# 1/den sent to the channels through DRAM, a narrow Gram tail and token sums, and a new order, in a kernel that joins a long convolution and a linear attention block

## The chip, the cores and the metric

One Trainium2 chip, one core. The metric is the device time of one execution in microseconds. Five engines run side by side, each through its own list of instructions in order: TensorE (PE in the profile; its weight loads are shown as PEld), VectorE (DVE), ScalarE (ACT), GpSimd (POOL) and SyncE (SP), which here issues every DMA. Matmul results go to PSUM, eight banks that this kernel uses as four pairs; an evicting instruction on ACT or DVE copies them to SBUF.

## The reference

Two independent parts, whose outputs stand side by side. `S = 2048` tokens, `D = 576` channels, 32 heads of 18 channels, all inputs bf16.

```python
# part A
k_shift = sum over t of k_pad[:, t:t+S, :] * shift_k[:, ks-1-t]        # 4 taps
kv = k_shift * v
y  = irfft(rfft(kv, 2S) * rfft(ssm_k, 2S))[:S] + kv * ssm_D            # causal convolution
A  = q * y
# part B
q, k, v = split(x @ wqkv)                                              # 32 heads of 18
phi = lambda t: where(t > 0, t + 1, exp(t)) + 1e-6
kv  = einsum("bhsd,bhse->bhde", phi(k), v)
z   = phi(k) summed over tokens
num = einsum("bhqd,bhde->bhqe", phi(q), kv)
den = einsum("bhqd,bhd->bhq", phi(q), z)[..., None] + 1e-6
B   = (num / den) joined over heads @ wo
```

## The kernel before

Part A is cut into five chunks of channels (four of 128, one of 64). A chunk's convolution is two stages of small Fourier matmuls over 16 x 128 token indices, forward for the taps (`h`) and for `kv` (`u`), a product, and two stages back. In the names of the order list: `hl`/`hd`/`hT` load a chunk of `ssm_k`, add `ssm_D` to its first tap and transpose it (on TensorE, or by a copy and a DMA transpose); `cv` is the four-tap shift and the multiply by `v`, on DVE or POOL; `h1`/`u1` are the first forward stage, `ht`/`ut` a DMA transpose of its result, `h2`/`u2` the second stage; `pX`, `pT`, `pS`, `pA` the complex product (`N` in place of an engine drops a sum, and `i1` then carries one more plane of matmuls); `i1`/`i2` the stages back, `i2` multiplying by `q` on DVE; `st` the store.

Part B: `xl` loads x, `xd` transposes it; `k` and `q`/`qt` project and apply phi (exp on ACT, min and max on DVE) into `pk` and into `pqT` (channels 0 to 511 by tokens) and `pq4` (channels 512 to 575, two token groups on the two halves of the partitions). Instead of projecting v, the kernel makes the Gram product `GT = x^T phi(k)` (`G.0` to `G.4`, 16 token blocks each), then `kv` from `wv^T GT`, kept block diagonal by head, then `M = kv wo` (`M.0` to `M.4`), so that the output is `(phi(q) / den) @ M` (`o`, eight units of two 128-token blocks). `G.4` has 64 channels of x and a column of ones (`x_sb` is 577 wide, unit `one`), so that its 65th row holds the token sums z. `den` multiplies phi(q) by z spread over heads, adds epsilon and takes the reciprocal on DVE: `rden`, 32 heads on each of four partition groups (one group of 512 tokens each). `bc.c.gg` spreads it from heads to channels: two matmuls with the selecting matrix `esel` (built by eight POOL selects in `hc`), then one DVE instruction that computes `(pqT + eps) * spread` straight from PSUM; `bt` does the same for `pq4`.

The order of everything is written out by hand in the list `ORDER`: units run in that order on every engine's own list, and the digits behind a slash name the PSUM bank pair or the SBUF slot that a tile takes. A unit that waits, waits in its place, and so does whatever is queued behind it on that engine. SP issues all loads, stores and DMA transposes in the same order.

The lines that the change touches: the constants (L103 to L114, L132, L205 to L212, L233), the x tile (L308 to L316), L602, `b_G` (L619), `b_kv` (L631), `b_M` (L653), `b_den` (L668), `b_bc` (L690), `b_bt` (L699), `b_out` (L708). L292 and L294 are the helper that evicts on ACT and on DVE.

## Time and profile before

| | us |
|---|---|
| three runs, median (lowest to highest) | 171.63 (169.48 to 173.51) |
| the profiled execution, its own time | 171.69 |
| its span, first to last instruction | 170.0 |
| granted TensorE clock, mean | 0.976 of full |
| ACT busy | 123.6 (73%) |
| POOL busy | 93.1 (55%) |
| DMA queue of SP: 31.61 MB | 84.8% of 16 engines' span |

The busy time of TensorE comes from records of pipelined matmuls: the duration in a row of one matmul (379 ns for 512 columns) is longer than its spacing in a stream, so prices are read from start to start. A row of the timeline shows the start, the duration (of the whole run where it says x16), engine, line, operation, output and inputs, and in brackets the idle time before it and what ended it.

### The profile page before, as it was taken

Reading aid. Unit: us, or ns where it says so; the run is one execution under the profiler, and the core shown is the slowest. Engines: PE = TensorE matmul, PEld = TensorE weight load, DVE = VectorE, ACT = ScalarE, POOL = GpSimd, SP = SyncE. Lnnn points to the kernel's source line nnn. Section 1 sums busy time; section 2 is a strip of 40 time slices with the busy share of each in tenths; the row PEclk is TensorE's granted clock in tenths of the full one; section 3 lists DMA queues with packets and bytes.
Section 4 is the critical chain, followed back from the end, with each engine's and each line's share of the span. In section 5 each row is a group of like instructions: output and inputs, shape, how many; then the busy total and the mean of one; then the engine's idle time right before and its main releaser. Section 6 shows DMA issues by size and latency. Waiting matters only on the chain. (4 is left out here: it accounts for less than half of the span.)

```text
span 170.0 us, 4572 instructions
## 1 busy us (share of the span) xinstructions
PE 154.7 (91%) x1975; PEld 97.2 (57%) x1975; DVE 146.2 (86%) x163; ACT 123.6 (73%) x142; POOL 93.1 (55%) x80
## 2 busy tenths in 40 slices
PE   7598999999999899999959999978999989969990
PEld 7496554565634573545565578665546555647650
DVE  7787499988899899999999968696998989998861
ACT  3459998887898878505679967978998777675111
POOL 7996109459919799997000029999994050505000
PEclk9969999999999999999978999999999999999998
DMA  3899949999989699899997611984669999580586
GB/s 124 254 357 304 260 98 230 320 182 183 217 208 156 152 230 167 149 259 242 245 233 191 123 28 25 184 188 139 127 123 183 222 242 142 155 267 9 183 271 133
DMA packets 79564, 31.90 MB, mean 188 GB/s; under 512 B 55294, under 2 KB 78840, under 8 KB 79544
## 3 DMA queue, kind: packets, MB, share of 16 engines
q1 hardware_dynamic: 79544, 31.61, 84.8%
q8 instruction: 15, 0.25, 0.6%
q14 instruction: 5, 0.04, 0.1%
HBM read 15.48 MB, written 4.72 MB: 119 GB/s over the span
## 5 line engine op out<-in xcount | busy, mean ns | idle before, releaser
L544 POOL TENSOR_TENSOR T<-T 128x1024 bf16<-128x1024 bf16 x5 | 11.3, 2255 | 21.0 <-DVE T L541 20.9
L424 PE MATMUL k_ps<-wqk,xT 128*128 128x512 bf16 (+1 forms) x160 | 20.9, 286 | 0.0
L625 PE MATMUL g_ps<-pk,x_sb 128*128 128x65 bf16 (+3 forms) x160 | 20.6, 287 | 0.3 <-ACT SU L292 0.3
L504 PEld LDWEIGHTS <-G 128*128 128x128 bf16 x320 | 17.6, 97 | 5.0 <-issue 3.6
L433 PE MATMUL q_ps<-xT,wqk 128*128 128x512 bf16 x80 | 18.4, 379 | 0.0
L463 DVE TENSOR_TENSOR at<-at 128x2048 bf16<-128x2048 bf16 (+1 forms) x13 | 17.0, 1308 | 1.0 <-POOL at L462 0.5
L462 POOL TENSOR_TENSOR at<-k,Wj 128x2048 bf16<-128x2048 bf16 (+1 forms) x4 | 14.3, 3580 | 6.1 <-DVE at L463 3.4
L292 ACT ACTIVATE Cu<-s_ps 128x1024 bf16<-128x1024 f32 (+1 forms) x17 | 15.8, 978 | 1.9 <-PE s_ps L504 1.7
L718 PE MATMUL o_ps<-wo_M,pqT 128*128 128x512 bf16 (+1 forms) x128 | 17.0, 286 | 0.1
L292 ACT ACTIVATE SU<-s_ps 128x1024 bf16<-128x1024 f32 x16 | 15.8, 1021 | 1.7 <-PE s_ps L527 1.3
L625 PEld LDWEIGHTS <-x_sb 128*128 128x128 bf16 (+1 forms) x160 | 10.9, 101 | 10.8 <-issue 1.5
L292 ACT ACTIVATE ob<-o_ps 128x576 bf16<-128x576 f32 x12 | 7.4, 650 | 13.2 <-PE o_ps L723 13.2
L424 PEld LDWEIGHTS <-xT 128*128 128x128 bf16 x160 | 10.9, 98 | 10.4 <-issue 0.5
L561 PE MATMUL i_ps<-W,T 64*128 64x128 bf16 x160 | 12.4, 234 | 4.3 <-ACT wv_GT L629 1.9
L292 ACT ACTIVATE T<-s_ps 128x1024 bf16<-128x1024 f32 x16 | 15.8, 1019 | 0.7 <-PE s_ps L527 0.6
L292 ACT ACTIVATE Ch<-s_ps 128x1024 bf16<-128x1024 f32 (+1 forms) x16 | 14.6, 948 | 2.3 <-PE s_ps L504 2.3
L292 ACT ACTIVATE V<-i_ps 128x1024 bf16<-128x1024 f32 x14 | 13.6, 1027 | 1.1 <-DMA Ctu<-Cu 0.9
L417 DVE SCALAR_TENSOR_TENSOR pk<-pk,k_ps 128x576 bf16<-128x576 bf16 x16 | 11.9, 753 | 2.9 <-ACT pk L416 2.9
L416 ACT ACTIVATE pk<-k_ps,neg 128x576 bf16<-128x576 f32 x16 | 11.8, 745 | 3.6 <-PE k_ps L424 3.4
L539 POOL TENSOR_TENSOR X<-SU,T 128x2048 bf16<-128x2048 bf16 x3 | 13.0, 4331 | 1.6 <-ACT SU L292 1.6
L718 PEld LDWEIGHTS <-pqT 128*128 128x128 bf16 x128 | 8.7, 98 | 8.5 <-issue 0.5
L462 DVE TENSOR_TENSOR at<-k,Wj 128x2048 bf16<-128x2048 bf16 (+1 forms) x11 | 13.1, 1187 | 0.2 <-POOL at L463 0.2
(144 smaller groups left out, 363.2 us busy)
## 6 DMA issues: line engine op xcount, KB each, us to landing
x_sb<-in_B_x_dram SPq DMA_DIRECT2D x4, 576.0 KB, 7.4
out_dram<-ob SPq DMA_DIRECT2D x8, 288.0 KB, 2.3
h_sb<-in_A_ssm_k_dram SPq DMA_DIRECT2D x4, 512.0 KB, 5.1
k<-in_A_k_dram SPq DMA_DIRECT2D x2, 1024.0 KB
v<-in_A_v_dram SPq DMA_DIRECT2D x2, 1024.0 KB
q<-in_A_q_dram SPq DMA_DIRECT2D x2, 1024.0 KB
out_dram<-q SPq DMA_DIRECT2D x2, 1024.0 KB
wqk<-in_B_wqkv_dram SPq DMA_DIRECT2D x2, 576.0 KB, 8.2
```

The lines of the kernel that those rows point to most:

```text
L292: nc.scalar.activation(out=out, in_=in_, func=ACT.Copy)
L416: nc.scalar.activation(out=out_ap, in_=ps_ap, func=ACT.Exp, bias=K.neg1[0:n, :])
L417: nc.vector.scalar_tensor_tensor(out=out_ap, in0=out_ap, scalar=1.0, in1=ps_ap, op0=ALU.min, op1=ALU.max)
L424: nc.tensor.matmul(ps[:, n0:n1], lhsT=xT[r // 4][:, t, rr * 128:(rr + 1) * 128], rhs=wqk[:, t, D + n0:D + n1], start=(t == 0), stop=(t == 4))
L433: nc.tensor.matmul(ps[:, j, :], lhsT=wqk[:, t, 128 * c:128 * c + 128], rhs=xT[g][:, t, :], start=(t == 0), stop=(t == 4))
L462: on[0].tensor_tensor(out=t_, in0=kk[:, 3 - stage:19 - stage], in1=wb(stage), op=ALU.mult)
L463: on[1].tensor_tensor(out=a_, in0=a_, in1=t_, op=ALU.add)
L504: nc.tensor.matmul(ps[:, bi, 0:dc], lhsT=K.G[ri][:, b, :], rhs=xf(b), start=True, stop=True)
L539: e.tensor_tensor(out=s['X', hf][:], in0=s['SU', hf][:], in1=t[:, :, ::-1, :], op=ALU.mult)
L561: nc.tensor.matmul(ps[:, r, g, :], lhsT=s[key, hf][64 * r:64 * r + 64, z, x, 128 * g:128 * g + 128], rhs=K.W[64 * r:64 * r + 64, m, :], st ...
L625: nc.tensor.matmul(ps[0:fn, n0:n1], lhsT=x_sb[:, r, f0:f0 + fn], rhs=pk[:, r, n0:n1], start=(r == 0), stop=(r == 15))
L718: nc.tensor.matmul(ps[:, n0:n1], lhsT=pqT[:, c, r * 128:(r + 1) * 128], rhs=B['M'][:, c, n0:n1], start=(c == 0), stop=False)
```

## The change

It moves the spreading of 1/den off TensorE: `rden` is stored to a scratch tensor in DRAM (`rs`), and five loads (`bl`) read it back, each head's row repeated for its 18 channels, into two rotating buffers (the slots of `xT`, free by then); a DVE multiply of two SBUF operands (`bc`) follows. Epsilon is added to phi(q) beforehand (`ep`, four times on ACT, once on DVE). `esel` and its eight selects go, and `ones`. The Gram tail `G.4` has 64 columns, even token blocks on the lower half and odd ones on the upper half of the output partitions; the token sums are a unit of their own, `z`, in four 32-column tiles. The tail of `wv` is loaded twice so that the kv products run over 128 rows everywhere, and `M`'s second product over all rows of the next head chunk. An `f` behind a unit `o` runs its tail matmuls first.

`ORDER` is written anew. Units that now run otherwise: `hT.2` and `hT.3` by a POOL copy and a DMA transpose, `hT.4` on TensorE, `hT.1` evicted by ACT; nine sums dropped (`N`) in place of four; no `pX`, `pS` on POOL; all `o` evictions on ACT; 56 warm-up matmuls in place of 40. From the reciprocal to the first `o` the new list reads:

```
den/3 cv.3.3.PPD u2.2.0.1.A/11 pA.1.0.N u2.2.0.0.A/2 i1.1.0.1.A/00 ht.3.1/1 i1.1.1.1.A/1 i1.1.1.0.A/2 pX.2.1.D/0
i1.1.0.0.A/0 cv.4.0.D hT.4.D/12 cv.4.1.DP ht.3.0/0 rs h2.3.1.1.A/33 vl.2/1 u1.3.1.0.A/12 u1.3.1.1.A/0 u1.3.0.1.D/3
u1.3.0.0.A/1 i2.1.1/2 h2.3.1.0.A/0 pX.2.0.D/1 M.1.A/3 bl.2/1 bc.2.D bl.4/0 bc.4.D i2.1.0/1 pA.2.0.N h2.3.0.0.A/22
h1.4.0.0.A/00 pT.2.0.D h2.3.0.1.A/3 h1.4.1.0.A/2 ut.3.1/1 M.2.A/0 pS.2.0.N M.4.A/3 pT.2.1.D ut.3.0/0 cv.4.2.DD
h1.4.0.1.A/2 u2.3.1.0.D/11 u2.3.1.1.A/0 bl.3/1 bc.3.D pS.2.1.N bl.1/0 h1.4.1.1.A/3 pA.2.1.N M.3.A/2 i1.2.0.1.A/10
cv.4.3.PDD i1.2.0.0.A/3 pX.3.1.D/1 bc.1.D M.0.A/2 u2.3.0.0.A/00 i1.2.1.0.A/1 u2.3.0.1.A/3 ht.4.0/1 i1.2.1.1.A/2
u1.4.1.1.A/00 u1.4.0.0.D/1 bl.0/1 h2.4.0.1.A/13 bc.0.D u1.4.1.0.A/2 ql.1/0 u1.4.0.1.A/0 pX.3.0.D/0 pA.3.0.P
h2.4.0.0.A/1 ql.2/0 pT.3.0.D i2.2.1/3 pA.3.1.D pS.3.0.D ut.4.0/0 o.1.0.AAf/20
```

```diff
-    K.esel = cpool.tile([128, D], BF, name="esel")
...
-    K.onesr = cpool.tile([128, 8], BF, name="onesr")
...
+    K.onec = cpool.tile([128, 32], BF, name="onec")
...
-        nc.sync.dma_start(out=wg[0:64, 0, 4, :], in_=wqkv[512:576, 2 * D:3 * D])
+        for i in range(2):
+            nc.sync.dma_start(out=wg[64 * i:64 * i + 64, 0, 4, :], in_=wqkv[512:576, 2 * D:3 * D])
...
+    def evict_G(ps, out):
+        ex = ab.tile([128, 1], FP32, name="ex", tag="ex", bufs=2)
+        nc.vector.tensor_copy(out=ex[:], in_=ps[:, D:D + 1])
+        nc.scalar.activation(out=out, in_=ps[:, 0:D], func=ACT.Identity, bias=ex[:])
...
+                if t < 4:
+                    nc.tensor.matmul(ps[:, n0:n1], lhsT=x_sb[:, r, 128 * t:128 * t + 128], rhs=pk[:, r, n0:n1],
+                                     start=(r == 0), stop=(r == 15))
+                else:
+                    h = slice(64 * (r % 2), 64 * (r % 2) + 64)
+                    nc.tensor.matmul(ps[h, n0:n1], lhsT=x_sb[:, r, 512:576], rhs=pk[:, r, n0:n1], start=(r < 2),
+                                     stop=(r > 13))
+        evict_G(ps, B['GT'][:, t, :])
+
+    def b_z():
+        ps = psum.tile([128, 1024], FP32, name="zs_ps")
+        for n0, n1 in ((0, 512), (512, 577)):
+            for r in range(16):
+                j = 32 * (r % 4)
+                nc.tensor.matmul(ps[j:j + 32, n0:n1], lhsT=K.onec[:], rhs=pk[:, r, n0:n1], start=(r < 4), stop=(r > 11))
+        B['zs'] = ab.tile([128, D], BF, name="zs")
+        evict_G(ps, B['zs'][:])
...
-    def b_bc(c, gg):
-        ps = psum.tile([128, 2, 512], FP32, name="bc_ps")
...
+    def store_r():
+        B['rs'] = dpool.tile([32, 4, 512], BF, name="rscr")
+        nc.sync.dma_start(out=B['rs'][:].rearrange("h j n -> j h n"), in_=B['rden'])
+
+    def eps_q(c, eng='A'):
+        p = pqT[:, c, :] if c < 4 else pq4[:]
+        if eng == 'A':
+            nc.scalar.activation(out=p, in_=p, func=ACT.Identity, bias=K.epsc[:])
+        else:
+            e = nc.gpsimd if eng == 'P' else nc.vector
+            e.tensor_scalar(out=p, in0=p, scalar1=EPS, scalar2=None, op0=ALU.add)
+
+    def load_r(c):
+        t = B['bc', c] = ring([128, 5, 512], BF, "rb", "xT", 2)
+        jobs = [(0, 0, 4, min(128, D - 128 * c))]
+        if c == 4:
+            jobs = [(64 * i, PAIR[0][i], 2, 64) for i in range(2)]
+        for p0, j0, jn, n in jobs:
+            ch = 128 * c
+            end = ch + n
+            while ch < end:
+                h, e = divmod(ch, 18)
+                m, k_ = (1, min(18 - e, end - ch)) if e or end - ch < 18 else ((end - ch) // 18, 18)
+                src = B['rs'][h:h + m, j0:j0 + jn, :].rearrange("h j n -> h (j n)")
+                nc.sync.dma_start(out=t[p0:p0 + m * k_, 0:jn, :].rearrange("p j n -> p (j n)"),
+                                  in_=src.unsqueeze(1).to_broadcast([m, k_, 512 * jn]))
+                p0 += m * k_
+                ch += m * k_
+
+    def b_bc(c, eng='D'):
+        p, r = (pqT[:, c, :], B['bc', c][:, 0:4, :]) if c < 4 else (pq4[:], B['bc', c][:, 0:2, :])
+        if c < 4:
+            r = r.rearrange("p j n -> p (j n)")
+        (nc.gpsimd if eng == 'P' else nc.vector).tensor_tensor(out=p, in0=p, in1=r, op=ALU.mult)
```

More of the change, by code (lines that the diff above doesn't have):

```diff
@@ L311, in load_x @@
     def load_x(g):
[L312 to L315 removed]
+        nc.sync.dma_start(out=x_sb[:, 4 * g:4 * g + 4, :], in_=xv[:, 4 * g:4 * g + 4, :])
     def xt(g):
@@ L713, in b_out, with tail @@
-        for r in rs:
-            ps = psum.tile([128, 1024], FP32, name="o_ps")
-            pss.append(ps)
+        pss = [psum.tile([128, 1024], FP32, name="o_ps") for r in rs]
+        first = len(eng) > 2
+        def tail():
+            for n0, n1 in ((0, 512), (512, 576)):
+                for i in range(2):
+                    h = slice(64 * i, 64 * i + 64)
+                    nc.tensor.matmul(pss[i][:, n0:n1], lhsT=pq4[h, p, rr * 128:(rr + 1) * 128], rhs=B['M'][h, 4, n0:n1],
+                                     start=first, stop=not first)
@@ L725, in b_out @@
+        if not first:
+            tail()
+        if eng[2:] == 's':
+            evict(B['ob'][:, rs[0], :], pss[0][:, 0:D], eng[0])
+            nc.sync.dma_start(out=outB[:, rs[0], D:2 * D], in_=B['ob'][:, rs[0], :])
+            for n0, e in ((0, 'D'), (288, 'A')):
+                evict(B['ob'][:, rs[1], n0:n0 + 288], pss[1][:, n0:n0 + 288], e)
+            nc.sync.dma_start(out=outB[:, rs[1], D:2 * D], in_=B['ob'][:, rs[1], :])
+            return
         for i, r in enumerate(rs):
```

141 lines of the change are left out of this document (53 added, 88 removed).

## The prediction

> **What bounds the kernel now.** I read the page's busy times first, then the timeline of TensorE for the places where it stands still, then the waits that explain those places, and last the timeline of VectorE against the order list.
>
> ```profile
> span 170.0 us, 4572 instructions
> PE 154.7 (91%) x1975; PEld 97.2 (57%) x1975; DVE 146.2 (86%) x163; ACT 123.6 (73%) x142; POOL 93.1 (55%) x80
> 165.91 0.75 DVE ob L294
> ```
>
> Two engines are nearly full. No engine's sum alone is the time: TensorE (PE) and VectorE (DVE) hold each other up. The chain of waits ends with the last output eviction on DVE, and behind that only the store, until 170.0. Of TensorE's 15.3 idle us, some 4 lie at the end, where only the eviction and the store run. Two places before that matter for this change.
>
> The first is at 85 us:
>
> ```profile
> 83.62 1.18 PE L482 MATMUL hT_ps<-ident,h_sb 128*128 128x128 bf16 x16
> 86.73 0.25 PE L561 MATMUL i_ps<-W,T 64*128 64x128 bf16 x2 [1.94 <-ACT wv_GT L629]
> ...
> 90.22 4.17 PE L625 MATMUL g_ps<-pk,x_sb 128*65 128x512 bf16 x32
> 94.33 0.63 PE L527 MATMUL s_ps<-Cth,W 64*32 64x512 bf16 x16
> ...
> 140.04 0.23 PE L561 MATMUL i_ps<-W,T 64*128 64x128 bf16 x2
> 141.04 2.13 PE L718 MATMUL o_ps<-wo_M,pqT 128*128 128x512 bf16 x16
> ACT wv_GT L629 <- DVE ex L628: 9.6, 3, 5.9
> 75.19 1.54 POOL L109 TENSOR_SCALAR_AFFINE_SELECT esel<-esel 32x576 bf16<-32x576 bf16 x1
> 76.23 1.57 DVE L462 TENSOR_TENSOR at<-k,Wj 128x2048 bf16<-128x2048 bf16 x1
> 77.83 3.03 DVE L463 TENSOR_TENSOR at<-at 128x2048 bf16<-128x2048 bf16 x1
> 80.89 1.22 DVE L462 TENSOR_TENSOR at<-k,Wj 128x2048 bf16<-128x2048 bf16 x1
> ```
>
> TensorE waited 1.94 us for a Gram eviction on ScalarE (ACT), which itself waited up to 5.9 us for the one-column copy `ex` on DVE. DVE was late because its elementwise operations took 1.57 us and once 3.03 us where the same shape takes 1.22; the long ones stand beside GpSimd's `esel` selects, and the 3.03 beside another small GpSimd operation. After the wait the four i1 units (64 matmuls) from 86.73 to 90.22 took 3.49 us; two units of the same kind at 140.04 to 141.04 took 1.0, so four cost 2.0 at full speed. The place costs 1.94 + 1.5 = 3.4 us.
>
> The second is the stretch from the denominators to the first output block:
>
> ```profile
> 107.75 1.05 PE L672 MATMUL den_ps<-pqT,zsel 128*32 128x512 bf16 x16
> 109.26 0.62 PE L527 MATMUL s_ps<-Ctu,W 64*32 64x512 bf16 x16
> 109.75 0.76 DVE L686 TENSOR_SCALAR den_ps<-den_ps,ez 128x512 f32<-128x512 f32 x1
> 110.54 3.36 DVE L688 RECIPROCAL wo_M<-den_ps 128x512 bf16<-128x512 f32 x1
> ...
> 130.59 1.22 DVE L697 SCALAR_TENSOR_TENSOR pqT<-pqT,bc_ps 128x1024 bf16<-128x1024 bf16 x1
> 132.00 2.13 PE L718 MATMUL o_ps<-wo_M,pqT 128*128 128x512 bf16 x16
> ```
>
> The last multiply by 1/den ends at 131.81 and the first output matmul starts at 132.00: DVE's chain sets it, not TensorE's own work. So the span is three pieces: 109.26 us up to the end of `den` on TensorE, 22.74 us from there to the first `o`, and 38.0 us after it.
>
> **Up to `den`.** The tail of the Gram product ran 32 matmuls from 90.22 to 94.33, 4.1 us. In 64-column pairs it should take half:
>
> ```profile
> 53.43 1.27 PE L441 MATMUL qt_ps<-xT,wqk 128*64 128x512 bf16 x10
> 54.63 0.41 PE L527 MATMUL s_ps<-Ctu,W 64*32 64x512 bf16 x8
> 58.97 1.16 PE L482 MATMUL hT_ps<-ident,h_sb 128*128 128x128 bf16 x16
> 60.06 0.41 PE L527 MATMUL s_ps<-Ctu,W 64*32 64x512 bf16 x8
> ```
>
> Here ten 64-column matmuls of 512 took 1.20 us, 0.24 a pair, so two do run side by side: -2.05. The new token sums are 16 matmuls of 512 and 16 of 65 in 32-column tiles; the 16 of `den` took 0.98 us (107.75 to 108.73), and the 65-wide ones are taken at 0.02 each: +1.3. The head transposes of chunks 2 and 3 leave TensorE for a GpSimd copy and a DMA transpose: 58.97 to 60.06 is 1.09, 83.62 to 84.80 is 1.18, -2.27. One i1 pair gets a third plane because its subtraction is dropped (pS.0.1.N): two units at 0.5 / 2 more, about +0.4 rounded with its weights. Sum -2.6.
>
> The wait at 85 us should go. Without `esel` and with the `X` and `S` sums off GpSimd, the DVE stretches of five operations by 0.35 and one by 1.8 have no cause: DVE is some 3.5 us less behind, while the added `ex` copy is short. Count -3.4; both ends are 0 and -3.4. What covers this: `pq + eps` now runs on ScalarE (four times; one on DVE), which has idle time there (73% busy). If that cover is missing, the evictions of the Gram product queue behind it and the wait returns.
>
> ```profile
> 119.21 4.07 POOL L541 TENSOR_TENSOR T<-SU,T 128x2048 bf16<-128x2048 bf16 x1
> 120.96 4.64 DVE L697 SCALAR_TENSOR_TENSOR pqT<-pqT,bc_ps 128x1024 bf16<-128x1024 bf16 x4
> 1.15 4.18 PE L80 MATMUL warm_ps<-sm 128*128 128x128 bf16 x40 [1.15 <-DVE sm L82]
> ```
>
> The two GpSimd copies for the transposes may stretch DVE as the selects did. No row shows such a copy, so they cost 0 to +2.4 us (some seven operations by 0.35); I take 0, since four DVE operations beside GpSimd's 4.07 us product took 4.64, no more than without it. Sixteen more warm-up matmuls lie in the shadow of the first loads: 0, at most 16 x 4.18 / 40 = 1.7. The padded kv rows change no matmul's length: 0. The first piece becomes 109.3 - 6.0 = 103.3.
>
> **From `den` to the first `o`.** DVE's own queue counts here. Per operation:
>
> ```profile
> L695 PE MATMUL bc_ps<-wo_M,esel 32*128 32x512 bf16 x16 | 3.1, 384 | 0.0
> 88.08 1.22 DVE L460 TENSOR_TENSOR at<-k,Wj 128x2048 bf16<-128x2048 bf16 x1
> ...
> 95.21 1.21 DVE L462 TENSOR_TENSOR at<-k,Wj 128x2048 bf16<-128x2048 bf16 x1
> 131.73 0.68 DVE L462 TENSOR_TENSOR at<-k,Wj 128x1024 bf16<-128x1024 bf16 x1
> ...
> 134.38 0.69 DVE L463 TENSOR_TENSOR at<-at 128x1024 bf16<-128x1024 bf16 x1
> ```
>
> The spreading matmuls free 3.1 us of TensorE, and the four of the tail some 0.4, but TensorE isn't the bound here, so that alone gains nothing. Six full DVE operations from 88.08 to 95.21 are 1.19 each start to start, four half ones 0.66. Between the reciprocal and the first `o` the new order has 14 full ones (four of them the new multiplies, bf16 from SBUF) and 9 half ones: 16.7 + 5.9 = 22.6 us. With 0.2 of lead and 0.76 + 3.36 for the reciprocal the piece is 26.9 us against 22.74: **+4.2**. The multiplies themselves got cheaper (five of 5.4 us in place of nine of 11), but convolution, products and evictions of chunks 2 to 4 were moved in front of them.
>
> The added waits. The sync queue (SP) now stores 1/den, then loads it back in 15 pieces, and DVE waits for each chunk; queued behind a waiting multiply are the DVE products and the evictions that free PSUM banks, and TensorE waits for those.
>
> ```profile
> h_sb<-in_A_ssm_k_dram SPq DMA_DIRECT2D x4, 512.0 KB, 5.1
> out_dram<-ob SPq DMA_DIRECT2D x8, 288.0 KB, 2.3
> k<-in_A_k_dram SPq DMA_DIRECT2D x2, 22.5 KB, 1.6
> 112.98 3.32 SPq L617 DMA_DIRECT2D wo_M<-in_B_wo_dram  x5
> ```
>
> A 512 KB load lands 5.1 us after its issue; a smaller store, 2.3; an issue takes 3.32 / 5 = 0.66. First multiply: 2.3 + two issues 1.3 + 5.1 = 8.7 against 5 full and 3 half operations of cover, 7.9: wait 0.8. Chunk 3, whose buffer is freed by the first multiply: 1.3 + 5.1 = 6.4 against four full and three half, 6.7: none. Chunk 0, freed by chunk 3: 0.66 + 5.1 = 5.8 against two full and three half, 4.4: 1.4. Together **+2.2**; the ends are 0 and, with fewer DMA engines per load, 15 (below). TensorE's own work in the stretch is at most 22.7 - 3.5 and the 5.0 that are moved in (next part), 24.2 us of 29.1, so it will stand still about 5 us in it; the half-speed loss behind the 1.94 us wait was 1.5, and I take half of that, **+0.75**.
>
> The Trainium skill's page "TensorE: Matmul & The Clock Gate", Part 1, says the clock halves after an idle window of about 3.4 us and needs as long a busy one to come back: by it this loss would be an estimated 1.7 us in place of 0.75, and the trace's loss after only 1.94 us of waiting is earlier than the page has it.
>
> **From the first `o` on.** Ahead of it now lie eleven units that lay behind: two u2 and two h2, four u1 of chunk 4, two i1, one i2.
>
> ```profile
> 136.83 0.41 PE L527 MATMUL s_ps<-Ctu,W 64*32 64x512 bf16 x8
> 137.18 0.86 PE L504 MATMUL s_ps<-v,G 128*128 128x64 bf16 x16
> 137.97 0.41 PE L527 MATMUL s_ps<-Ctu,W 64*32 64x512 bf16 x8
> L292 ACT ACTIVATE ob<-o_ps 128x576 bf16<-128x576 f32 x12 | 7.4, 650 | 13.2 <-PE o_ps L723 13.2
> ```
>
> At 0.35, 0.40, 0.5 and an estimated 0.95 each that is 1.4 + 1.6 + 1.0 + 0.95: **-5.0**, hidden ahead of `o` by the DVE chain. The last pair of blocks is evicted by ScalarE twice, 1.3 us in place of 0.75: **+0.55**.
>
> Sum: -6.0 + 4.2 + 2.2 + 0.75 - 5.0 + 0.55 = -3.3, made against the profiled execution's 171.69 us (span 170.0 and 1.69 around it), which is also the median of the runs (171.63): **168.4 us**. DVE is left with eleven full and seven half operations behind the first `o`, 17.7 us of the 33.5, so nothing new should appear there.
>
> **Rivals.** *Everything hides* (0.24). The loads land under cover and TensorE's wait is split so that its clock holds: 168.4 - 2.2 - 0.75 = 165.4. For it: each cover misses by about 1 us only. Against: other transposes stand ahead in the same queue.
>
> *The loads come late* (0.20), the one that ends slower. Place: DVE at the first, third and last multiply. The main piece of a load reads six or seven head rows and repeats them 18 times; if so few rows use so few of the 16 DMA engines, the data part of 5.1 - 1.6 = 3.5 us grows by about 16/6 on 84% of the bytes (seven on 98%: the same 7.9), landing 9.5 us after issue. Waits: 5.2, 4.1 and 5.8, 15.1 in place of 2.2, 181.3 in all; with half the excess and the clock's whole loss, 175.6. I take 176.5. It is slower than before by 2% once the three waits exceed 9 us. For it: nothing in the old trace repeats rows like this.
>
> The Trainium skill's page "DMA: Bandwidth & Descriptors", section "Why a DMA increments its semaphore by 16 and not by 1", says a DMA uses the largest number up to 16 that divides the slowest dimension of both sides, here 6 or 7; at its 27 GiB/s per engine a load is an estimated 1.6 us longer, which alone would give about 173. No row here shows it.
>
> *The early gain doesn't come* (0.14). The wait at 85 us stays for want of DVE time: 168.4 + 3.4 = 171.8; if narrow tiles did not overlap either, 2.05 + 2.8 more, 176.7. The `qt` row speaks against the latter, so 172.5. That the change doesn't do what it says is this case.
>
> **How the numbers follow.** The forecast has 0.42, with its own range 166 to 171. About 2% (168.2 and 175.1) is what a measurement tells from no change; the forecast lies on that line, 0.20 of it faster and 0.22 the same. Faster: 0.20 + 0.24 = 0.44. Same: 0.22 + 0.14 + 0.02 of the late loads = 0.38. Slower: 0.18. The range runs from 163.5 (everything hides and the small gaps before `o` go too) to 176.5, which leaves out half of the late loads and a little below.
>
> **What would show it.** Right: `den` on TensorE ends near 103 to 105 us; DVE operations stay at 1.2 us between 60 and 85; the first `o` starts 29 us after `den`, and TensorE idles several us before it; the first and last multiplies wait a microsecond for DMA; 33 us follow. Wrong: Gram tail matmuls spaced as before; a half-speed stretch of i1 again; landings of the spread loads near 9 us; or a first `o` that starts earlier than DVE's list allows, which would mean the half operations are cheaper than 0.66.

## The result and the profile after

| | before | after |
|---|---|---|
| median of the runs, us | 170.78 (169.48 to 173.51, 4 runs) | 189.50 (188.21 to 189.79, 4 runs) |
| ratio, 95% interval | | 1.111 (1.100 to 1.122) |
| profiled execution, its own time, and span | 171.69, 170.0 | 189.79, 188.0 |

The forecast was 168.4 with a range to 176.5; the changed kernel is 11% slower. Ratios leave out executions that took over 1.5% longer than the fastest of the same kernel; medians and ranges hold all of them. From the page of the changed kernel:

```profile
span 188.0 us, 4745 instructions
PE 157.7 (84%) x2047; PEld 100.9 (54%) x2047; DVE 141.5 (75%) x158; ACT 128.9 (69%) x150; POOL 61.9 (33%) x64
...
PEclk9988999999999999999969999996579669789998
```

The engines have little more to do than before: TensorE is busy 3 us longer, part of it at a lower clock (PEclk is the granted clock in tenths of full speed), ScalarE 5 us longer, VectorE 5 and GpSimd 31 us shorter. The time went into waiting. The windows view, cut where the prediction cut the span (end of `den` on TensorE, first full output matmul, end), shows in which piece. Columns: stretch, its length, then busy time and count of each engine, granted clock, DMA share, GB/s. The kernel before:

```profile
0.00:109.26 109.26, 102.15 (x1135) 64.58 (x1136) 95.51 (x113) 83.19 (x92) 66.04 (x71) 0.97 0.91 198
109.26:132.00 22.74, 20.67 (x390) 12.90 (x381) 19.91 (x18) 20.43 (x26) 20.01 (x7) 1.00 0.79 152
132.00:170.00 38.00, 31.87 (x467) 19.75 (x464) 30.73 (x33) 19.94 (x27) 7.02 (x3) 0.98 0.75 179
```

The changed kernel, the same view:

```profile
0.00:111.15 111.15, 100.66 (x1171) 62.70 (x1172) 94.02 (x115) 86.89 (x95) 50.06 (x60) 0.97 0.98 209
111.15:151.35 40.20, 27.86 (x536) 20.79 (x528) 26.00 (x26) 27.34 (x35) 4.24 (x2) 0.83 0.86 157
151.35:188.00 36.65, 29.13 (x348) 17.40 (x348) 21.45 (x18) 14.66 (x21) 7.55 (x2) 0.88 0.58 157
```

The forecast's pieces were 103.3, 29.9 (22.74 + 4.2 + 2.2 + 0.75) and 33.55 us. Measured: 7.85, 10.3 and 3.1 more, 21.25 in sum, which is the miss (188.0 against 168.4 - 1.69). In the middle piece VectorE works 26.0 of 40.2 us. Its timeline there, the rows that wait:

```profile
126.78 1.23 DVE L725 TENSOR_TENSOR pqT<-pqT,rb 128x2048 bf16<-128x2048 bf16 x1 [4.00 <-DMA rb<-rscr]
130.70 0.69 DVE L725 TENSOR_TENSOR pq<-pq,rb 128x1024 bf16<-128x1024 bf16 x1 [2.70 <-DMA rb<-rscr]
140.10 1.23 DVE L725 TENSOR_TENSOR pqT<-pqT,rb 128x2048 bf16<-128x2048 bf16 x1 [2.84 <-DMA rb<-rscr]
150.07 1.23 DVE L725 TENSOR_TENSOR pqT<-pqT,rb 128x2048 bf16<-128x2048 bf16 x1 [3.96 <-DMA rb<-rscr]
```

Four of the five multiplies wait, 13.5 us together against 2.2 in the forecast. SyncE's queue at that time (a row covers as many issues as it says, with their waits):

```profile
116.13 0.64 SPq L694 DMA_DIRECT2D rscr<-wo_M  x1
...
120.21 5.50 SPq L716 DMA_DIRECT2D rb<-rscr  x7
125.89 7.10 SPq L503 DMA_TRANSPOSE Ctu<-Cu  x2
133.10 4.47 SPq L716 DMA_DIRECT2D rb<-rscr  x6
137.67 5.58 SPq L503 DMA_TRANSPOSE Cth<-Ch  x1
143.43 1.44 SPq L716 DMA_DIRECT2D rb<-rscr  x2
```

Loads and transposes of chunks 3 and 4 take turns, and each holds up the other: the loads of chunks 3 and 1 are issued from 133.10 on, behind two transposes, that of chunk 0 at 143.43, behind a third. Behind the first output block, and before `den`, another kind of row stands out:

```profile
100.87 4.07 POOL L454 TENSOR_TENSOR at<-k,Wj 128x2048 bf16<-128x2048 bf16 x1
103.00 3.02 DVE L533 TENSOR_TENSOR T<-SU,T 128x2048 bf16<-128x2048 bf16 x1
...
155.63 4.50 POOL L533 TENSOR_TENSOR T<-SU,T 128x2048 bf16<-128x2048 bf16 x1
156.14 4.53 DVE L536 TENSOR_TENSOR T<-T 128x1024 bf16<-128x1024 bf16 x1
...
160.73 0.23 PE L553 MATMUL i_ps<-W,T 64*128 64x128 bf16 x2 [2.39 <-DVE T L536]
```

VectorE operations of 1.2 and 0.7 us last 3.02 and 4.53: each ends about one of its own lengths after the end of the GpSimd operation that was running when it began (104.94 and 160.13). TensorE waits 2.39 us for the second.

### The profile page after: what moved, and what is told of

Read it like the earlier page. It is cut to its first block, busy times and chain, and to the rows that moved or that the text cites. A ratio compares the mean times of both kernels' runs of the same rounds, so it can differ in the third digit from the quotient of the medians.

```text
span 188.0 us, 4745 instructions
## 1 busy us (share of the span) xinstructions
PE 157.7 (84%) x2047; PEld 100.9 (54%) x2047; DVE 141.5 (75%) x158; ACT 128.9 (69%) x150; POOL 61.9 (33%) x64
## 4 chain that ended last, share of the span: by engine, by line
PE 40%; DMA 22%; DVE 20%; SPq 5%; POOL 4%; issue 4%; ACT 3%; ACTq 0%; DVEq 0%; POOLq 0%
PE k_ps L416 8%; PE q_ps L425 7%; PE o_ps L746 7%; DMA rb<-rscr 6%; DMA q<-in_A_q_dram 5%; PE s_ps L496 4%; PE g_ps L623 4%; DMA k<-in_A_k_dram 4%; SPq L716 3%; POOL sm L182 3%; DMA Ctu<-Cu 3%; DVE q L568 3%; DMA Cth<-Ch 2%; DVE T L536 2%; DVE T L533 2%
## 5 line engine op out<-in xcount | busy, mean ns | idle before, releaser
L287 ACT ACTIVATE ob<-o_ps 128x576 bf16<-128x576 f32 x16 | 10.0, 652 | 18.3 <-PE o_ps L738 10.8
L746 PE MATMUL o_ps<-wo_M,pqT 128*128 128x512 bf16 (+1 forms) x128 | 18.7, 306 | 1.9 <-DVE pqT L725 1.9
L287 ACT ACTIVATE SU<-s_ps 128x1024 bf16<-128x1024 f32 x13 | 13.1, 1024 | 9.7 <-PE s_ps L519 6.6
L623 PE MATMUL g_ps<-pk,x_sb 128*128 128x512 bf16 (+1 forms) x128 | 17.8, 299 | 0.1
L455 POOL TENSOR_TENSOR at<-at 128x2048 bf16<-128x2048 bf16 (+1 forms) x3 | 11.5, 3826 | 19.1 <-DVE at L454 19.0
L553 PE MATMUL i_ps<-W,T 64*128 64x128 bf16 x224 | 15.1, 233 | 2.5 <-DVE T L536 2.4
L416 PEld LDWEIGHTS <-xT 128*128 128x128 bf16 x160 | 11.0, 98 | 10.4 <-issue 0.5
L553 PE MATMUL i_ps<-W,X 64*128 64x128 bf16 x208 | 15.2, 234 | 1.7 <-issue 1.7
L287 ACT ACTIVATE V<-i_ps 128x1024 bf16<-128x1024 f32 x14 | 13.8, 1038 | 2.8 <-PE i_ps L553 2.7
L482 POOL COPY hp<-h_sb 128x2048 bf16<-128x2048 bf16 x2 | 7.9, 3952 | 22.6 <-PE s_ps L496 20.9
L496 PE MATMUL s_ps<-hT,G 128*128 128x128 bf16 (+1 forms) x160 | 11.3, 222 | 4.8 <-DVE hT L289 2.4
L455 DVE TENSOR_TENSOR at<-at 128x2048 bf16<-128x2048 bf16 (+1 forms) x12 | 13.6, 1134 | 1.6 <-POOL at L454 1.2
```

Source lines behind the costliest of these rows:

```text
L287: nc.scalar.activation(out=out, in_=in_, func=ACT.Copy)
L416: nc.tensor.matmul(ps[:, n0:n1], lhsT=xT[r // 4][:, t, rr * 128:(rr + 1) * 128], rhs=wqk[:, t, D + n0:D + n1], start=(t == 0), stop=(t == 4))
L455: on[1].tensor_tensor(out=a_, in0=a_, in1=t_, op=ALU.add)
L482: nc.gpsimd.tensor_copy(out=hp, in_=hv)
L496: nc.tensor.matmul(ps[:, bi, 0:dc], lhsT=K.G[ri][:, b, :], rhs=xf(b), start=True, stop=True)
L553: nc.tensor.matmul(ps[:, r, g, :], lhsT=s[key, hf][64 * r:64 * r + 64, z, x, 128 * g:128 * g + 128], rhs=K.W[64 * r:64 * r + 64, m, :], st ...
```

## Experiments

Each was run beside the kernel before. "Pieces" are the three stretches of the profiled execution; after has 111.15 + 40.20 + 36.65. Of the long lines of `ORDER`, the diffs show only the units that change. One thing to hold against every small difference: in kernels whose order up to `den` is the same as after's, the first piece ran between 107.55 (f3_nopool) and 111.15 us (after), in e2_poolq for 112.46, and no run shows why.

### The loads moved, split and replaced

**Loads in own buffers, all behind the store (e1_hoist).**

```diff
-        t = B['bc', c] = ring([128, 5, 512], BF, "rb", "xT", 2)
+        if 'rb' not in B:
+            B['rb'] = big.tile([128, 16, D], BF, name="rb", tag="x")[:].rearrange("p r n -> p (r n)")
+        t = B['bc', c] = B['rb'][:, 2048 * c:min(2048 * c + 2048, 9216)].rearrange("p (j n) -> p j n", n=512)
...
-rs h2.3.1.1.A/33 vl.2/1
+rs bl.2 bl.4 bl.3 bl.1 bl.0 h2.3.1.1.A/33 vl.2/1
...
-bl.2/1 bc.2.D bl.4/0 bc.4.D
+bc.2.D bc.4.D
...
```

> The five loads of 1/den get buffers of their own (in the room that x leaves) and are all issued right behind the store, ahead of the two DMA transposes of chunk 3 and the one of chunk 4. Theory Q (the loads come late because of their places in SP's queue): in the changed kernel DVE waited 4.0 + 2.7 + 2.8 + 4.0 = 13.5 us for them; here the waits before chunks 3, 1 and 0 go, about 7 remain before chunks 2 and 4, and the time is 181 to 184. Theory E (each load is slow by itself, since it runs on few DMA engines): five loads in a row on the same engines take 18 us, the last two multiplies still wait, 186 or more. Theory N (the new order is slow whatever happens to 1/den): less than 2 us gained.

Measured: 193.14 us (192.34 to 195.54), pieces 110.44 + 46.48 + 35.18. Slower than after. The timeline of this kernel, SyncE and one row of TensorE:

```profile
119.33 11.23 SPq L718 DMA_DIRECT2D rb<-rscr  x15
130.60 0.64 SPq L386 DMA_DIRECT2D v<-in_A_v_dram  x1
132.65 10.74 SPq L503 DMA_TRANSPOSE Ctu<-Cu  x2
143.48 1.06 PE L519 MATMUL s_ps<-Ctu,W 64*32 64x512 bf16 x16 [18.28 <-DMA Ctu<-Cu]
```

Theory Q's 181 to 184 failed. The multiplies wait less for loads (6.5 us in place of 13.5), and the wait moves: the chunk 3 transposes, 11 us of issues later, keep TensorE idle for 18.28 us.

**Loads on GpSimd's queue (e2_poolq):** `nc.sync.dma_start` becomes `nc.gpsimd.dma_start` in `store_r` and `load_r`, with the buffers of e1.

> The store and the loads of 1/den are issued by POOL instead of SP, with buffers of their own, at the old places of the order. SP then issues transposes and other loads only. Theory Q: 178 to 182, better than with the loads hoisted on SP, because the transposes of chunks 3 and 4 aren't delayed by 16 issues of 0.7 us. Theory E: 184 to 187. Theory N: 187 or more. If POOL's own issue is slow (over 1 us each), the waits come back.

Measured: 191.96 us (189.46 to 194.23), ratio 1.121 (1.097 to 1.144). Theory Q's 178 to 182 failed, too. The loads left SyncE's queue for GpSimd's list, and that is no free queue either:

```profile
120.81 2.12 POOL L455 TENSOR_TENSOR at<-at 128x1024 bf16<-128x1024 bf16 x1 [9.55 <-DVE at L454]
122.88 0.95 POOL L694 DMA_DIRECT2D rscr<-wo_M  x1
```

The store, issued at 116.13 in the changed kernel, stands behind a GpSimd step of chunk 4's convolution, which waits 9.55 us for VectorE; the first multiply waits 11.88 us. What a queue without other work would give is not shown.

**1/den stored twice (e3_two),** so that a load's slowest dimension has 12 or 14 rows in place of 6 or 7:

```diff
-        B['rs'] = dpool.tile([32, 4, 512], BF, name="rscr")
-        nc.sync.dma_start(out=B['rs'][:].rearrange("h j n -> j h n"), in_=B['rden'])
+        B['rs'] = dpool.tile([32, 2, 4, 512], BF, name="rscr")
+        for i in range(2):
+            nc.sync.dma_start(out=B['rs'][:, i].rearrange("h j n -> j h n"), in_=B['rden'])
...
-                src = B['rs'][h:h + m, j0:j0 + jn, :].rearrange("h j n -> h (j n)")
+                w = 2 if k_ == 18 else 1
+                src = B['rs'][h:h + m, 0:w, j0:j0 + jn, :].rearrange("h i j n -> (h i) (j n)")
...
-                                  in_=src.unsqueeze(1).to_broadcast([m, k_, 512 * jn]))
+                                  in_=src.unsqueeze(1).to_broadcast([w * m, k_ // w, 512 * jn]))
```

> The scratch tensor holds every head's row twice (two stores), and the main piece of each load reads 12, 14 or 6 rows instead of 6, 7 or 3; nothing else moves. Theory E: the packets of the main piece, 3.4 us on about six engines at once in the changed kernel's trace, take 1.8; the piece of chunk 4 4.5 -> 2.3; the four waits of 13.5 us shrink by 6 to 8, time 182 to 184. Theory Q: the data time isn't what is waited for; one more issue, 188 to 191.

Measured: 186.22 us (184.64 to 186.98), pieces 110.62 + 37.30 + 36.38; the middle is 2.9 shorter, and the four waits sum to 10.4 in place of 13.5 us, half of what theory E expected. By the trace's packets the main piece of a load (115 packets of 4 KB) took 3.4 us in the changed kernel with 5.8 packets in flight on average, an `h_sb` load of 112 such packets in the kernel before 1.5 us with 13.8 (others had 9 to 12); stored twice, 2.36 us with 9.9. The Trainium skill's page "DMA: Bandwidth & Descriptors", section "Why a DMA increments its semaphore by 16 and not by 1", says that the slowest dimension bounds the number of engines; the trace agrees (six rows, 5.8 in flight). It was worth some 3 of the 19 us.

**Matmul spreading in the new order (e4_matmul):** store and loads out, `esel`, `bc` and `bt` as in the kernel before, epsilon still added beforehand, PSUM banks for them chosen by hand:

```diff
-bl.2/1 bc.2.D bl.4/0 bc.4.D
+bc.2.0/0 bc.2.1/2 bt/3
...
-bl.3/1 bc.3.D
+bc.3.0/1 bc.3.1/3
...
-bc.1.D
+bc.1.0/2 bc.1.1/0
...
-bc.0.D
+bc.0.0/2 bc.0.1/0
```

> In the new order 1/den is spread by matmuls from the selecting matrix again (built on POOL beside the reciprocal), multiplied from PSUM on DVE, epsilon still added beforehand; no store, no loads. Theories Q and E, for which the DRAM route is the whole loss between den and the first output: the first output block starts 24 to 28 us behind den instead of 40, 174 to 178 in all. Theory N: the first part (den ends at 111 instead of the forecast 103) stays, and so do the waits of chunk 3 and 4 transposes: 180 or more.

Measured: 188.88 us (188.12 to 189.99), pieces 109.10 + 45.10 + 32.10. No faster, so at this point the new order itself looked guilty. The windows of its middle piece say more:

```profile
109.10:154.20 45.10, 32.95 (x556) 23.57 (x548) 34.39 (x32) 28.07 (x35) 12.04 (x11) 0.76 0.53 100
```

VectorE has 34.4 us of work there against 26.0, and TensorE ran at 0.76 of its clock. Its matmuls take turns with other units at the PSUM pairs that I chose, where TensorE waits up to 2.44 us at a time for VectorE's multiplies. So this run is no clean undoing; it shows that the old route does not fit into the new order, not what the new route costs.

**Multiplies and loads later (g2_late),** on the kernel f3 below, with the buffers of e1:

```diff
-ut.3.0/0 cv.4.2.DD
+ut.3.0/0 bl.2 bl.4 cv.4.2.DD
...
-u2.3.1.1.A/0 bl.3/1 bc.3.D pS.2.1.N bl.1/0 h1.4.1.1.A/3
+u2.3.1.1.A/0 bl.3 pS.2.1.N h1.4.1.1.A/3 ht.4.0/1 bl.1 bl.0
...
-pX.3.1.D/1 bc.1.D
+pX.3.1.D/1 bc.2.D bc.4.D
...
-u1.4.0.0.D/1 bl.0/1
+u1.4.0.0.D/1 bc.3.D bc.1.D bc.0.D
```

> The changed kernel without the two GpSimd products of chunk 3 (182.0 by itself), and with the spread loads in buffers of their own, issued behind the chunk 3 transposes of u and h, and the five multiplies at the end of VectorE's list ahead of the first output block. Nothing else is moved. Theory L (what the stretch from den to the first output block lost, 40.8 us against a forecast of 29.9, is VectorE's waits for loads, 11.6 us there): the waits fall below 4 us in sum, the first full output matmul comes 33 to 36 us after den's end and the time is 175 to 178. Rival U (VectorE's waits for the loads cover waits for the transposes of chunk 3 and their matmuls, which are late by themselves): the waits move to other operations, the first output stays 38 us or more behind den, the time 180 to 182.5.

Measured: 186.78 us (183.75 to 187.59; 183.75 is the profiled run), pieces 108.06 + 41.62 + 32.32. Theory L failed: the first output comes 41.62 us after `den`, as rival U has it, and even its lowest time is above f3's median of 181.98. The multiplies were not all covered, though: VectorE still waits 8.5 us for loads, where theory L wanted less than 4. The waits of TensorE in its middle piece (in all, times, longest):

```profile
PE s_ps L518 <- DMA Cth<-Ch: 8.1, 2, 7.7
PE o_ps L747 <- DVE pqT L726: 6.7, 1, 6.7
```

The wait went to the transposes of chunk 4, now behind ten loads, and to the last multiply.

**Both stores, later multiplies and ex on ScalarE (g3_comb).**

> The kernel of g2_late with two more edits: ex on ScalarE, and 1/den stored twice so that a load's slowest dimension has 12 or 14 rows. If the causes are separate and add up (ex -1.9, two copies up to -3.3, less where the loads are covered already): 171 to 174. If they overlap: no better than g2_late by more than 1 us. If it falls below 168.5 it is the first version faster than the kernel before.

Measured: 179.84 us (178.30 to 180.36), ratio 1.051 (1.042 to 1.060), pieces 110.31 + 35.66 + 32.73. The three edits do not add up to the 171 to 174 expected. Beside the profiled run of g2_late (183.75) the gain is 3.9 us, near the 3.3 that the second copy gave by itself; TensorE's wait for the chunk 4 transposes falls from 7.69 to 4.93.

**The DRAM route alone in the old order (g4_dram).**

```diff
-        nc.vector.scalar_tensor_tensor(out=p, in0=p, scalar=EPS, in1=ps[:], op0=ALU.add, op1=ALU.mult)
+        (nc.gpsimd if eng == 'P' else nc.vector).tensor_tensor(out=p, in0=p, in1=r, op=ALU.mult)
...
-lwo
+lwo rs
...
-ht.3.1/0
+ht.3.1/0 bl.1 bl.3
...
-bt/0 ut.3.0/0
+ut.3.0/0 bl.2 bl.4 bl.0
...
-bc.0.0/1
+bc.1.D bc.3.D bc.2.D bc.4.D bc.0.D
```

> The kernel before in its own order, with the spreading of 1/den alone replaced by the store and 15 loads through DRAM (buffers of their own, in the space of x) and five multiplies on VectorE in place of nine. It leaves out the addition of 1e-6 to pq before the multiply, and the esel tile. Store behind the output weights' loads, loads of chunks 1 and 3 behind the chunk 3 transposes of h, the others behind those of u. Theory Q (round trip and places on the sync queue bound it): 1/den at 113.9, store down at 118.5, the last loads issued to about 137 and down at 142, the first output block at 142 to 145 against 132.0, the time 178 to 184. Rival C (the route is cheap by itself, and only the new order and its GpSimd work cost): the first output block by 136, the time 169 to 174.

Measured: 186.38 us (185.83 to 188.45), ratio 1.093 (1.083 to 1.102), pieces 107.02 + 40.72 + 39.06. Rival C is out, and the loss is above theory Q's range, too: in the old order, which was made for the other route, the middle grows from 22.7 to 40.7 us, though VectorE's work in it falls from 19.9 to 15.0. TensorE waits 12.72 us there for the last multiply.

**No spreading at all (h1_noload).**

```diff
-rs
...
-bl.2/1 bc.2.D bl.4/0 bc.4.D
+bc.2.D bc.4.D
...
-bl.3/1 bc.3.D pS.2.1.N bl.1/0
+bc.3.D pS.2.1.N
...
-bl.0/1
...
-        (nc.gpsimd if eng == 'P' else nc.vector).tensor_tensor(out=p, in0=p, in1=r, op=ALU.mult)
+        nc.vector.tensor_tensor(out=p, in0=p, in1=p, op=ALU.mult)
```

> The changed kernel without the store and the 15 loads; the five multiplies stay where they are on VectorE, and multiply pqT by itself. It leaves out the spreading of 1/den. Theory L (the loads are the cause in the stretch, by VectorE's waits for them, 13.5 us, and by the transposes that stand behind them on the sync queue): the first full output matmul comes 28 to 31 us after den's end, as the forecast had it without waits, and the time is 177 to 180. Rival U (the chunk 3 chain and VectorE's list in the new order are late by themselves, as the matmul route in that order suggests, with 44 us): 35 us or more after den, the time 184 to 188.

Measured: 175.42 us (173.01 to 177.18). This settles the middle piece. The windows:

```profile
0.00:109.93 109.93, 100.10 (x1171) 62.13 (x1172) 93.79 (x115) 86.88 (x95) 49.94 (x60) 0.97 0.98 211
109.93:137.25 27.32, 23.93 (x535) 18.44 (x528) 27.11 (x26) 26.58 (x35) 4.26 (x2) 1.00 0.93 155
137.25:173.20 35.95, 27.38 (x352) 16.38 (x348) 21.25 (x18) 14.88 (x22) 7.56 (x2) 0.93 0.52 149
```

VectorE works 27.11 of 27.32 us: its list is the piece, as the prediction had it, and TensorE keeps its full clock. The store and 15 loads cost 14.1 us (189.50 - 175.42); between the two profiled spans it is 14.8, of which 12.9 lie in this piece. Rival U is out. SyncE's transposes in this run:

```profile
119.91 5.19 SPq L502 DMA_TRANSPOSE Ctu<-Cu  x2
127.32 3.10 SPq L502 DMA_TRANSPOSE Cth<-Ch  x1
```

Behind the loads these three held the queue for 7.10 and 5.58 us, with 1/den stored twice (e3_two) for 4.95 and 3.80. That the loads lengthen the transposes is not shown by this: without any such load, the pair took 7.76 us in e4_matmul and the transpose of chunk 4 5.57 in the kernel before.

### GpSimd beside VectorE

**Two products of chunk 3 on VectorE (f3_nopool).**

```diff
-pX.3.0.D/0 pA.3.0.P
+pX.3.0.D/0 pA.3.0.D
...
-o.0.1.AAf/01 pT.3.1.P
+o.0.1.AAf/01 pT.3.1.D
```

> The changed kernel with the two GpSimd products of chunk 3 (4.07 and 4.50 us) on VectorE. Theory L (VectorE and GpSimd shut each other out when both read two operands from SBUF: the 128x1024 product of 4.53 us beside the 4.50 us of GpSimd is one operation of 0.7 us that waited): the longest VectorE product behind the first output block is below 1.4 us, TensorE's idle 2.39 us behind it goes, the part from the first output block to the end falls from 32.4 to about 30, and the time by 2 to 4, to 185.5 to 187.5. Rival V (VectorE is full there, too): the two added products cost the 1.2 us each that GpSimd spared, and the time stays within 1 us of 189.5 or rises.

Measured: 181.98 us (181.34 to 186.43), ratio 1.069 (1.057 to 1.081), pieces 107.55 + 40.75 + 31.20. Theory L: the last piece falls by 5.5 to

```profile
148.30:179.50 31.20, 25.77 (x343) 15.81 (x346) 18.34 (x20) 14.63 (x21) 0.00 (x0) 0.99 0.68 182
```

VectorE, with two operations more, is busy for 18.34 us in place of 21.45, and TensorE has its clock back (0.99 against 0.88). The rest of the gain lies before any edited instruction (the first piece is 3.6 us shorter), within that piece's scatter from kernel to kernel. The Trainium skill's page "SBUF — State Buffer", section "Who interferes with whom", says that a VectorE instruction with two SBUF inputs and a GpSimd instruction that reads SBUF exclude each other, the later one standing still until the first is done; the rows of 4.50 and 4.53 us, shown after the result, agree.

**The convolution of chunks 3 and 4 on VectorE, too (h4_cvd),** on h2_exnp below:

```diff
-cv.3.2.DP
+cv.3.2.DD
...
-cv.3.3.PPD
+cv.3.3.DDD
...
-cv.4.1.DP
+cv.4.1.DD
...
-cv.4.3.PDD
+cv.4.3.DDD
```

> The kernel of h2_exnp with the GpSimd steps of the convolutions of chunks 3 and 4 on VectorE, too, so that GpSimd does no elementwise work behind 80 us. Theory K (VectorE and GpSimd shut each other out there as well: a product of 1.2 us took 3.0 beside a GpSimd step): the stretched VectorE operations go, den ends 2 to 4 us earlier, the time is 1 to 4 us below h2_exnp. Rival V (VectorE has no room: the four full and two half steps are 6 us more on its list): the time is 2 to 6 us above h2_exnp.

Measured: 184.70 us (182.05 to 186.72), pieces 109.99 + 39.96 + 31.55; h2_exnp has 183.85. Neither theory: the stretched operation of 3.03 us goes, and VectorE, with four operations more in the middle piece, is busy 30.1 us there in place of 26.3.

### The part up to den

**ex on ScalarE in the changed kernel (f1_exact).**

```diff
-        nc.vector.tensor_copy(out=ex[:], in_=ps[:, D:D + 1])
+        nc.scalar.activation(out=ex[:], in_=ps[:, D:D + 1], func=ACT.Copy)
```

> The changed kernel with one edit: the one-column copy ex of each Gram eviction runs on ScalarE in place of VectorE. Theory X (the lost gain up to den is a relay: ex queued on VectorE, the Gram eviction wv_GT on ScalarE behind it, the chunk 1 transposes on the sync queue waiting 6.8 us for that, then the weight loads, F and the chunk 2 transposes behind those): the wait of 6.8 us shrinks below 2, TensorE's idle 3.20 us at 90.7 to 93.9 goes, den ends on TensorE 3 to 4.5 us earlier than 111.1, and the time falls from 189.5 to about 185 to 187. Rival V (VectorE's list is full in that stretch, and the relay only names its last link): another wait takes the place, den ends within 1 us of 111, the time stays at 188.5 to 190.5.

Measured: 187.64 us (186.96 to 188.93), between the two theories, pieces 108.28 + 40.44 + 36.58. TensorE's 3.20 us at 90 us became 1.79, but the chunk 1 transposes still held SyncE's queue for 10.38 us. **Together with f3 (h2_exnp):**

> The changed kernel with ex on ScalarE and without the two GpSimd products of chunk 3. If the two add up (-1.9 and -7.5): 179 to 181. If they overlap, or the 7.5 was partly an early part that happened to run well: 182 to 184.

Measured: 183.85 us (182.04 to 184.87), which is not below f3's 181.98. No effect of the copy is shown.

**The same in the kernel before (g1_exb).**

> The kernel before with one edit: the one-column copy ex of each Gram eviction runs on ScalarE in place of VectorE. It takes away the wait at 85 us, which the prediction priced at 3.4 us, without anything else of the change. Theory W (the copy behind VectorE's list is the cause of the wait and of the half clock behind it): no wait of over 0.5 us of TensorE for the Gram eviction there, i1 at full speed, den 2 to 3.4 us earlier than 109.3, the time 167.2 to 169. Rival V (what is behind is late too, or ScalarE's own queue takes the copy's place as the holder): den within 1 us of before, the time 170 to 171.5.

Measured: 172.03 us (170.17 to 172.05), ratio 1.004 (0.995 to 1.012). Rival V. At the place of the 1.94 us wait stands

```profile
85.96 0.23 PE L561 MATMUL i_ps<-W,T 64*128 64x128 bf16 x2 [1.65 <-DVE T L544]
...
87.09 0.29 PE L561 MATMUL i_ps<-W,T 64*128 64x128 bf16 x2 [0.51 <-DVE SU L294]
```

The Gram eviction is on time, and the next unit waits for VectorE's product instead.

**Narrow Gram tail and token sums alone, in the old order (f4_gram):** `b_G`, `b_z`, `evict_G`, the wv tail and the kv products as in the change, on the kernel before.

```diff
-one G.1/11
+G.1/11
...
-G.0/00 wom
+G.0/00 z/1 wom
```

> The kernel before with one part of the change alone: the Gram tail in 64-column tiles, the token sums in 32-column tiles with their own eviction, 128-row kv products; esel, the matmul spreading and the old order stay. By the prediction's terms (-2.05 for the tail, +1.3 for the sums) it is 0.75 us faster, 170.5 against 171.2. Rival (the sums need a place in PSUM, one more ex and one more eviction, on engines that are both behind there): the chain ex, eviction, i1 gets 0.7 to 1.5 us longer and the time is 171.5 to 173.

Measured: 173.03 us (172.04 to 173.37), ratio 1.017 (1.007 to 1.027), pieces 108.39 + 25.48 + 37.73. It comes out at the upper end of the rival's range, but at another place. TensorE's work up to `den` falls by about 2 us (102.15 to 100.00), `den` ends 0.7 sooner, measured at the same matmul, and the middle gives back 2.6, in waits for transposes above all (1.22 and 1.69 us).

**Head transposes of chunks 2 and 3 back on TensorE (f2_hTpe).**

```diff
-hT.2.p/12
+hT.2.D/12
...
-hT.3.p/21
+hT.3.A/31
```

> The changed kernel with the head transposes of chunks 2 and 3 back on TensorE (32 matmuls, 2.27 us) in place of a GpSimd copy and a DMA transpose. Theory P (what the prediction said: the move is free and TensorE is the bound up to den): den ends 2.3 us later, the time is 191 to 192. Rival T (the two GpSimd copies stretch VectorE and the DMA transposes of 2 to 3 us each hold the sync queue, so that the move cost more than it saved): den ends 0 to 2 us earlier and the time is 187 to 189.5.

Measured: 194.27 us (192.94 to 196.12), pieces 116.77 + 39.89 + 36.84. Rival T is out. The kernel is slower by more than theory P says, and only in part for its reason: up to `den` TensorE has 3.0 us more work (103.69 against 100.66, at 0.94 of the clock against 0.97) and stands still 2.6 us longer, once 3.87 us for ScalarE's eviction of `hT`.

**No loads, no GpSimd products, ex on ScalarE (h3_all).**

> The two edits of h2_exnp together with those of h1_noload. It leaves out the spreading of 1/den. By the forecast's own terms without the load waits, with den's end at the 108 us that these kernels have shown, 27.7 us for VectorE's list, 31.2 us from the first output block to the end (the length without GpSimd products) and 1.7 around the span: 168.6; Theory L says 167 to 172. Rival U: 174 to 178.

Measured: 170.48 us (169.26 to 172.79, 10 runs), ratio 1.005 (0.999 to 1.010), pieces:

```profile
0.00:110.97 110.97, 100.66 (x1171) 62.80 (x1172) 93.48 (x109) 87.57 (x101) 50.08 (x60) 0.97 1.00 209
110.97:138.27 27.30, 23.72 (x535) 18.37 (x528) 27.09 (x26) 26.63 (x35) 4.25 (x2) 1.00 0.84 156
138.27:169.50 31.23, 26.38 (x352) 16.02 (x348) 18.30 (x20) 14.73 (x22) 0.00 (x0) 0.99 0.60 170
```

With the spreading free of charge the new order only draws level: the last piece is 6.8 us shorter than before, the middle 4.6 longer, and the first, for which the forecast had 6 less, 1.7 longer.

**Weight loads and F behind the chunk 2 transposes, on h3_all (i1_front).**

```diff
-h1.2.0.0.A/3 lwv
+h1.2.0.0.A/3
...
-ep.0.A u2.1.0.0.D/0 FT.1.T cv.3.0.D
+ep.0.A u2.1.0.0.D/0 cv.3.0.D
...
-ht.2.1/1 ht.2.0/0
+ht.2.1/1 ht.2.0/0 FT.1.T
...
-ql.0/1
+ql.0/1 lwv
```

> The kernel of h3_all (170.5) with the six loads of wv and the second F transpose moved on the sync queue from ahead of the chunk 2 transposes of h to behind them. It leaves out the spreading of 1/den. Theory Q (those 6 us of issue hold the transposes, and the buffer of Cu with them): TensorE's idle 3.67 us at 90 us goes and the half-speed Gram tile of 5.2 us behind it runs in 4.1, den ends 4 to 5 us earlier than 110.97 and the time is 165.5 to 167. Rival V (the transposes wait for something else, matmuls or evictions): den within 1.5 us of 110, the time 169 to 171.

Measured: 171.00 us (169.10 to 172.55, 12 runs), pieces 108.74 + 29.94 + 31.02. The wait named by theory Q went (0.16 us left), and another came up in its place:

```profile
90.75 4.11 PE L623 MATMUL g_ps<-pk,x_sb 128*128 128x512 bf16 x31 [0.16 <-ACT Cu L287]
...
99.02 1.25 PE L645 MATMUL kv_ps<-wv_GT 128*128 128x126 bf16 x4 [2.05 <-DMA wv_GT<-in_B_wqkv_dram]
```

The moved loads were late themselves. `den` ended 2.2 us sooner, and the middle piece was 2.6 longer; the time did not move. VectorE works 28.88 of the 29.94 us there, on 28 operations in place of 26: the earlier `den` meets VectorE's list.

**All repairs with the spreading in place (i2_rep).**

> All repairs with the spreading in place: ex on ScalarE, no GpSimd products in chunk 3, the weight loads and F behind the chunk 2 transposes, 1/den stored twice. If the pieces add up (183.9 for the first two, -4 for the front, -3.3 for the second copy): 176 to 178, still slower than the kernel before. If the front repair is the cover of something late: 179 to 181.

Measured: 179.40 us (177.22 to 180.92), ratio 1.055 (1.048 to 1.062), pieces 109.60 + 36.95 + 31.15. The second alternative. With g3_comb it is the best complete version of the changed kernel, 10 us faster than after; none is below the kernel before.

## Why the prediction was wrong

**Up to den, -6.0: wrong, +1.9 in its place.** The matmul terms were near: the Gram tail took 2.18 us in f3's chain, the token sums 1.10, and putting `hT` back cost 3.0 us of TensorE's work for its 2.27. TensorE's work up to `den` fell from 102.15 to 100.66 us, where the forecast comes to 98.1 (102.15 - 2.6 - 1.5); part of the rest is half clock, below. The step that failed is "The wait at 85 us should go [...] Count -3.4". Its cause was named rightly, and VectorE's backlog did go: its full-size operations between 60 and 85 us last 1.2 us, ScalarE's Gram evictions wait 2.6 us in all for `ex` (9.6 before), and beside GpSimd's two copies (55 to 59 and 80 to 84 us) no VectorE operation is stretched. But what would be late next was not asked. The experiment on the kernel before shows what is: take the wait away and 1.65 us of another stands there. In the changed kernel TensorE is idle for 10.5 us up to `den` (111.15 - 100.66), where the forecast comes to 5.2 (7.1 before, less the 1.94), and the largest piece is this:

```profile
ACT wv_GT L615 <- DVE ex L614: 2.6, 3, 2.3
...
79.38 2.00 SPq L593 DMA_DIRECT2D wv_GT<-in_B_wqkv_dram  x4
81.43 1.15 SPq L595 DMA_DIRECT2D wv_GT<-in_B_wqkv_dram  x2
82.62 3.15 SPq L573 DMA_TRANSPOSE F<-G  x1
...
85.93 4.64 SPq L503 DMA_TRANSPOSE Cth<-Ch  x2
...
93.91 0.82 PE L496 MATMUL s_ps<-v,G 128*128 128x128 bf16 x8 [3.20 <-ACT Cu L287]
...
94.82 5.45 PE L623 MATMUL g_ps<-pk,x_sb 128*128 128x512 bf16 x32
...
100.38 0.16 DVE L614 COPY ex<-g_ps 128x1 f32<-128x1 f32 x1 [6.08 <-PE g_ps L623]
```

SyncE's queue, not VectorE, sets this place; VectorE itself stands still for 6.08 us until the Gram tile is done. The chunk 2 transposes stand behind six weight loads and the F transpose, the buffer of `Cu` behind them. The Gram tile that follows takes 5.45 us where others take 4.11. That the queue is the cause of this wait is shown by i1_front; that its repair pays is not. What makes up the rest of the 7.85 us stays open: the first piece differs by 3.6 us between after and f3_nopool, which have the same order there.

**den to the first output, +4.2 for VectorE's list: right.** Without the loads the piece is 27.32 us, at full clock; the forecast without its waits and the clock's loss is 22.74 + 4.2 = 26.9.

**The added waits, +2.2: the failed step that decided.** 13.5 us on VectorE, and 12.9 in the piece when the loads are left out; with VectorE's 26.0 us of work the waits fill 39.5 of the piece's 40.2 us. Term by term: the first multiply was to wait 0.8 and waited 4.00. The store was issued 0.8 us after the reciprocal's end and landed in 4.02 us, where 2.3 was taken from a store to the output; the cover was 7.4 in place of 7.9. The multiply of chunk 4 got no price and waited 2.70, since its four loads are issued behind the three of chunk 2. Chunk 3 was to wait "none" and waited 2.84, and chunk 0 was to wait 1.4 and waited 3.96, since transposes of 7.10 and of 5.58 us stand ahead of the one's loads and of the other's; the prediction counted issues of loads only, though it wrote that "other transposes stand ahead in the same queue". The landing it took, 5.1 us, was nearly right in spite of the few engines, as the chain of waits shows for two loads:

```profile
116.13 4.02 DMA rscr<-wo_M
...
125.00 5.58 DMA rb<-rscr
...
134.72 5.26 DMA rb<-rscr
```

**Half the clock's loss, +0.75.** In the same piece TensorE's busy time is 27.86 us at 0.83 of its clock, against 23.93 at full clock without the loads, with the same instructions: 3.9 us. It is hidden: VectorE's work and waits fill the piece.

**Behind the first output, -5.0 + 0.55: right in kind, and larger.** Without GpSimd's products the last piece is 31.2 us against 38.0, 6.8 less. But GpSimd's products got no price at all, and "nothing new should appear there" failed: they cost 5. The row by which the prediction took GpSimd's copies for harmless (four VectorE operations in 4.64 us beside a GpSimd product) reads one operand from PSUM, and beside the copies it held; the operations that were stretched read two from SBUF.

**Rivals.** "The loads come late" is the one that happened, at the place and, in its uncut sum of waits (15.1), near the measured 13.5. That is luck: its mechanism, a landing of 9.5 us, did not happen (5.26 and 5.58 above), and the sum was then halved to give 176.5. It had 0.20. "The early gain doesn't come" happened as well; the two were priced as alternatives and came together.

## What to carry to other kernels

A route through DMA is priced by its place in the queue: list every issue between the store and the last load, transposes and unrelated loads among them, and ask of each who waits for it, since loads that were pulled forward here only passed the wait on. A small stall that is removed can be counted only when the next late thing at that place has been named. A run that leaves the route out altogether prices it in one step, where moving its parts about left several readings. Before giving GpSimd elementwise work, look at how many SBUF operands VectorE reads beside it, not at whether GpSimd is idle.
